# Decay scans in one piece, 112-partition loads and split weight checks in an RWKV and gMLP kernel on one core

## The chip, the core and the metric

The kernel runs on one core of a Trainium2 chip. TensorE (PE) multiplies matrices, VectorE (DVE), ScalarE (ACT) and GpSimd (POOL) work on rows of 128 partitions, and SyncE (SP) issues most of the transfers from and to HBM. Each engine takes its own instructions in a fixed order and waits on semaphores for the others. The metric is the device time of one execution in microseconds, the median of several.

## The reference

The first part is a recurrent attention with 4 batches, 8 heads, 768 positions and 48 features per head; the second is a gated MLP on its output. Cut to what matters:

```
for t in range(S):                                  # attention, per batch and head
    cur = outer(u * k[t], v[t])
    y[t] = r[t] @ (state + cur)
    state = w[t][:, None] * state + outer(k[t], v[t])
x = y with the heads side by side                   # 4 x 768 x 384
h = gelu(x @ w_in);  u, v = halves of h             # tanh form, 512 columns each
v = (v - mean) / sqrt(var + 1e-6) * g_ln
v = einsum('ts,bsd->btd', w_sg, v) + b_sg           # a 768 x 768 weight along the positions
out = x + (u * v) @ w_out
```

## The kernel before

The attention runs in 24 chunks of 128 positions (4 batches of 6). Two heads share a tile: one on the partitions 0 to 47, one on 64 to 111; the partitions 48 to 63 and 112 to 127 hold nothing of the data. Four such pairs lie side by side in the columns. For each chunk SP loads W (the decays, 517 columns: in each pair 128 decays and a guard column), KR (k and r), the values, and k by token.

`decays(n)` makes two scans from W. A scan is one instruction that carries a value from column to column: new = in0 * old + in1, or with the operations that it is given. The first (L568) runs from the back and gives the suffix products in Suf; it is reset at each pair by the ones in `resets`, a PSUM tile. Then the reciprocals of Suf's first columns are taken, one for each pair (L574), and a second scan (L576) multiplies the decays forward from them; for the first eight chunks (`early`) this is done in two halves, for the later ones (L581, L583) in one piece with the reciprocals in an fp32 tile D2 that is zero elsewhere. `decays` then multiplies R by W (L617), `decayed_k` multiplies K by Suf (L585), and `own_weights` makes the diagonal: a product K*R (L629), matmuls with `u_col` (L634), a copy and eight scaled identity tiles (L653). `scores` (L678), `masked` (L755), `products` (L685), `outputs` (L701, L712) and `state` follow on PE and DVE. The scores and the first products of a chunk lie in one PSUM tile `a_ps`.

The MLP's matmuls are written as three each, of a value's high and low part in fp32r (L950 to L952). `f64_weight` splits the weights into these parts (L1303 to L1328), and `f64_check` looks at the weights' high words again: SP loads a piece, ACT takes the Square (L1339) and the Sign (L1340), each with a sum over the columns. `range_check` does the like for the decays. `verdict` (L1260) turns the sums into one flag, by small DVE instructions and one matmul (L1278). Each engine reads the flag (L1431), and when it is bad, a slower path follows in the program.

Everything is cut into steps, written as generators. The table ORDER lists one step after another by a letter for its kind, a number for its chunk or piece, and the engine; the class Plan runs through the table, so it sets the order of each engine's instructions, the order of the loads in SP's queue too. Plan also estimates times, and where PE would wait for more than 0.4 us by its estimate, it calls `fill`, which puts warm-up matmuls (L481, on a constant tile) there.

Of the kernel before, what the change touches and what calls it, by code (L numbers as in the profile page):

```python
# [1610 lines left out]
```

## Time and profile before

| | us |
|---|---|
| median of 3 runs | 348.34 (347.72 to 348.59) |
| the profiled execution | 350.2 |
| its span | 348.4, and 1.8 around it |
| PE busy in the span | 340.0 (98%) |
| DVE, ACT, POOL busy | 273.0 (78%), 213.5 (61%), 148.2 (43%) |
| mean granted PE clock | 0.987 of full speed |

Times in the rows are microseconds from the start of the span unless marked ns. A busy PE may be at either level of its clock, and a warm-up matmul counts as busy as well; the predicted times are therefore set against the medians, and the stretches against the rows. 0.3% of the time is 1.05 us.

### The profile page before, as it was taken

The numbers are of one execution on the slowest core, as the hardware profiler recorded it, in microseconds if no ns is written. First come the engines' busy times: TensorE is split into PE (matmuls) and PEld (weight loads), VectorE is DVE, ScalarE is ACT, GpSimd is POOL, SyncE is SP. The second block draws the span as 40 slices with busy tenths as digits, with TensorE's granted clock in tenths as the row PEclk, the third lists the DMA queues.
The fourth block names the chain that finished last, engine by engine and source line by source line (L and its number), as shares of the span: only waits on it lengthen the run. The fifth ranks groups of instructions, "written<-read, shape, count | busy, mean of one in ns | idle before, by whom it ended". The sixth has DMA issues, their size and how long they took to land.

```text
span 348.4 us, 10988 instructions
## 1 busy us (share of the span) xinstructions
PE 340.0 (98%) x4453; PEld 313.9 (90%) x4453; DVE 273.0 (78%) x541; ACT 213.5 (61%) x564; POOL 148.2 (43%) x221
## 2 busy tenths in 40 slices
PE   7999999999999999999999999999999999999994
PEld 6887688899999899889999989999999889999993
DVE  6989999998999799777889796866746365767673
ACT  1579799972664477572313375372642689897982
POOL 7356343505524541453707445144323634448400
PEclk9699999999999999999999999999999999999998
DMA  7868995614256737235256345220365454636742
GB/s 287 300 225 288 345 337 186 189 56 158 85 170 215 236 130 236 68 105 206 76 163 202 115 147 197 96 100 36 119 205 173 155 182 164 232 125 192 201 147 95
DMA packets 28470, 60.46 MB, mean 174 GB/s; under 512 B 3456, under 2 KB 13184, under 8 KB 28416
## 3 DMA queue, kind: packets, MB, share of 16 engines
q1 hardware_dynamic: 28272, 59.63, 51.5%
q8 instruction: 36, 0.59, 0.7%
q14 instruction: 18, 0.15, 0.2%
q10 hardware_dynamic: 144, 0.10, 0.1%
HBM read 53.82 MB, written 4.72 MB: 168 GB/s over the span
## 4 chain that ended last, share of the span: by engine, by line
PE 91%; ACT 3%; POOL 2%; DMA 2%; DVE 1%; issue 0%; SPq 0%; POOLq 0%; ACTq 0%
PE m_ps L950 17%; PE m_ps L952 16%; PE m_ps L951 16%; PE resets L950 6%; PE resets L951 6%; PE resets L952 6%; PE a_ps L678 5%; PE y_ps L701 4%; PE y_ps L712 3%; PE y_ps L685 2%; DMA x<-y 2%; PE m_ps L481 2%; PE m_ps L1145 1%; PE a_ps L1145 1%; PE m_ps L724 1%; PE y_ps L1145 1%
## 5 line engine op out<-in xcount | busy, mean ns | idle before, releaser
L950 PE MATMUL m_ps<-wsgh,vn 128*128 128x384 f32 x114 | 39.1, 343 | 0.0
L952 PE MATMUL m_ps<-wsgh,vn 128*128 128x384 f32 x114 | 38.4, 337 | 0.0
L951 PE MATMUL m_ps<-wsgl,vn 128*128 128x384 f32 x114 | 38.3, 336 | 0.0
L653 ACT ACTIVATE a<-KR,own 128x64 f32<-128x64 f32 x120 | 30.4, 342 | 4.1 <-DVE own L647 4.0
L617 POOL TENSOR_TENSOR KR<-KR,W 128x512 f32<-128x512 f32 x18 | 21.8, 1216 | 23.6 <-DVE W L568 8.1
L950 PE MATMUL m_ps<-g,wouth 128*128 128x384 f32 x80 | 27.3, 341 | 0.0
L952 PE MATMUL m_ps<-g,woutl 128*128 128x384 f32 x80 | 26.9, 336 | 0.0
L951 PE MATMUL m_ps<-g,wouth 128*128 128x384 f32 x80 | 26.9, 336 | 0.0
L1050 ACT CAST g<-m_ps 128x384 fp32r<-128x384 f32 x21 | 9.9, 477 | 27.0 <-DVE m_ps L1048 27.0
L950 PE MATMUL m_ps<-xT,winh 128*128 128x384 f32 x75 | 25.9, 345 | 0.0
L952 PE MATMUL m_ps<-xT,winl 128*128 128x384 f32 x75 | 25.2, 336 | 0.0
L951 PE MATMUL m_ps<-xT,winh 128*128 128x384 f32 x75 | 25.2, 336 | 0.0
L987 POOL TENSOR_TENSOR st<-st,mhalf 128x1 f32<-128x1 f32 x24 | 14.7, 613 | 20.2 <-DVE g L1322 6.3
L678 PE MATMUL a_ps<-KR 64*64 64x128 f32 (+1 forms) x768 | 22.8, 255 | 0.0
L1046 DVE SCALAR_TENSOR_TENSOR m_ps<-m_ps,flat 128x384 f32<-128x384 f32 x21 | 13.0, 618 | 12.1 <-PE m_ps L952 11.3
L950 PEld LDWEIGHTS m_ps<-wsgh,vn 128*128 128x128 f32 x114 | 21.4, 188 | 0.6
L583 DVE TENSOR_TENSOR_SCAN W<-W,D 128x516 f32<-128x516 f32 x16 | 21.4, 1337 | 0.4
L952 PEld LDWEIGHTS m_ps<-wsgh,vn 128*128 128x128 f32 x114 | 21.4, 188 | 0.3 <-DVE vn L1002 0.3
L701 PEld LDWEIGHTS y_ps<-a,vtok 64*64 64x64 f32 x768 | 16.0, 134 | 6.2 <-issue 3.9
L951 PEld LDWEIGHTS m_ps<-wsgl,vn 128*128 128x128 f32 x114 | 21.4, 188 | 0.2
L701 PE MATMUL y_ps<-a,vtok 64*64 64x64 f32 x768 | 21.2, 224 | 0.0
L585 POOL TENSOR_TENSOR KR<-KR,W 128x512 f32<-128x512 f32 x12 | 14.8, 1231 | 14.3 <-PE m_ps L952 3.7
(374 smaller groups left out, 1095.7 us busy)
## 6 DMA issues: line engine op xcount, KB each, us to landing
KR<-in_kr SPq DMA_DIRECT2D x24, 512.0 KB, 4.5
RK<-in_ktok SPq DMA_DIRECT2D x20, 384.0 KB, 4.2
W<-in_wpad SPq DMA_DIRECT2D x24, 258.5 KB, 3.1
KR<-in_wpad SPq DMA_DIRECT2D x9, 517.0 KB, 3.8
vtok<-in_vtok SPq DMA_DIRECT2D x24, 192.0 KB, 3.8
out<-o SPq DMA_DIRECT2D x21, 192.0 KB, 2.7
vn<-in_w_in SPq DMA_DIRECT2D x6, 512.0 KB, 4.8
KR<-in_w_in SPq DMA_DIRECT2D x6, 512.0 KB, 4.1
```

The lines of the kernel that those rows point to most:

```text
L583: nc.vector.tensor_tensor_scan(W[:, 0:WL - 1], W[:, 0:WL - 1], D2[:, 0:WL - 1], 0.0, ALU.mult, ALU.add)
L585: engine[op.e].tensor_tensor(cols(x.R), cols(x.R), blocks(W, 0), ALU.mult)
L617: engine[op.e].tensor_tensor(cols(x.K), cols(x.K), blocks(x.Suf, 2), ALU.mult)
L653: nc.scalar.activation(a[:, j, p], eyes, AF.Copy, scale=o[:, j, p:p + 1])
L678: nc.tensor.matmul(ps_[64 * c_:64 * c_ + 64, j, p * C:p * C + (2 * T if c_ < turn else T)], x.K[rows, at:at + T], r_, start=True, stop=True)
L701: m = nc.tensor.matmul(place(y, j, q, r, c_), x.V[64 * c_:64 * c_ + 64, h * D - up(p, j):h * D - up(p, j) + 64], x.a.tile[64 * c_:64 * c_ ...
L950: nc.tensor.matmul(ps, lh, rh, start=(i == 0), stop=False)
L951: nc.tensor.matmul(ps, lh, rl, start=False, stop=False)
L952: nc.tensor.matmul(ps, ll, rh, start=False, stop=(i == n - 1))
L987: nc.gpsimd.tensor_tensor(rstd, var, c.mhalf, ALU.pow)
L1046: nc.vector.scalar_tensor_tensor(ps, ps, c.g[:, d:d + 1], c.b_bc[:, ts], ALU.mult, ALU.add)
L1145: nc.tensor.matmul(ps, x, y, start=False, stop=True, skip_group_check=True)
```

## The change

Three edits, and a new table ORDER.

The second scan of each chunk becomes one instruction. The reciprocals are written into the guard columns of W itself (one instruction for all four pairs), and the scan gets a constant zero as its second operand, one element repeated: `r_zero` from the PSUM tile `resets` for the early chunks, `d_zero` from the bf16 tile D1 for the later ones. D2 is free of the decays then.

The ten weight checks become twenty of half the columns, and load into D2 (pool `s_d2`), from chunk 8 on, instead of into the buffers of KR after the last chunk. Of the decay checks only the first loads in two parts, before the first three.

W and, from chunk 2 on, KR are loaded on 112 partitions; two small casts on ACT clear the partitions 96 to 127 of two KR buffers at the start, and the elementwise work on W, K, R and the decayed state runs on 112 partitions (LIVE). The first warm-up has 16 matmuls instead of 11, `fill` takes the bank that came free first and counts from the time at which it is free, and the own-weights from chunk 2 on have no filler of their own.

```diff
+LIVE = 64 + D
...
-WARM = (11, 80.0, 0.22)
+WARM = (16, 80.0, 0.22)
...
-            self.fill(t - gap, int((gap - 0.15) / WARM[2]))
+            self.fill(t - gap, t)
...
-    r_two = resets[:, 0:HQ]
+    r_zero = resets[:, 0:1].broadcast_to([128, WL - 1])
     r_one = resets.bitcast(BF16)[:, 2 * HQ + WL - C - 2:2 * HQ - C - 1:-1]
     D1 = per.tile([128, WL], BF16, name="D1")
+    d_zero = D1[:, 1:2].broadcast_to([128, WL - 1])
-    nc.vector.memset(D2, 0.0)
...
+    for _, t in s_kr.free[2:]:
+        nc.scalar.copy(t[96:128, 0:2 * NP * C], D1[96:128, 1:2].broadcast_to([32, 2 * NP * C]))
...
-    def fill(t, n):
-
-        free = [x for at, x in m_m.free if at <= t]
-        if free:
-            warm(ident, n, free[0])
+    def fill(t, end):
+
+        if m_m.free:
+            at, bank = min(m_m.free, key=lambda x: x[0])
+            warm(ident, max(0, int((end - max(at, t) - 0.15) / WARM[2])), bank)
...
-        nc.sync.dma_start(ch[n].W[:, 0:WL], wpad[steps[n]])
+        nc.sync.dma_start(ch[n].W[0:LIVE, 0:WL], wpad[steps[n]][0:LIVE])
...
+        rows = 128 if n < 2 else LIVE
...
-        nc.sync.dma_start(t[:, 0:2 * NP * C], kr[b, g])
+        nc.sync.dma_start(t[0:rows, 0:2 * NP * C], kr[b, g][0:rows])
...
-        W, Suf = x.W, x.Suf
-        nc.vector.tensor_tensor_scan(Suf[:, WL - 1:0:-1], W[:, WL - 1:0:-1], r_one if early else D1[:, WL - 1:0:-1], 0.0,
+        W, Suf = x.W[0:LIVE], x.Suf[0:LIVE]
+        nc.vector.tensor_tensor_scan(Suf[:, WL - 1:0:-1], W[:, WL - 1:0:-1], (r_one if early else D1[:, WL - 1:0:-1])[0:LIVE], 0.0,
                                      ALU.mult, ALU.add)
-        if early:
-            for i in range(2):
-                at = slice(i * HQ, (i + 1) * HQ)
-                yield Op({"DVE": 0.1}, after=[ch[n - 1].e_pre] if n else [])
-                nc.vector.reciprocal(r_two[:, 0:HQ:Q], Suf[:, i * HQ + 1:(i + 1) * HQ:Q])
-                op = yield Op({"DVE": 0.64}, done=x.e_pre if i else None)
-                nc.vector.tensor_tensor_scan(W[:, at], W[:, at], r_two, 0.0, ALU.mult, ALU.add)
-            if n == RESETS - 1:
-                m_m.free.append((op.seen, resets))
-        else:
-            yield Op({"DVE": 0.12}, after=[ch[n - 1].e_pre] if n else [])
-            nc.vector.reciprocal(D2[:, 0:WL - 1:Q], Suf[:, 1:WL - 1:Q])
-            yield Op({"DVE": 1.17}, done=x.e_pre, two=True)
-            nc.vector.tensor_tensor_scan(W[:, 0:WL - 1], W[:, 0:WL - 1], D2[:, 0:WL - 1], 0.0, ALU.mult, ALU.add)
+        yield Op({"DVE": 0.12})
+        nc.vector.reciprocal(W[:, 0:WL - 1:Q], Suf[:, 1:WL - 1:Q])
+        op = yield Op({"DVE": 1.17}, after=[ch[i].e_pre for i in range(n)] if n == RESETS - 1 else [], done=x.e_pre,
+                      two=not early)
+        nc.vector.tensor_tensor_scan(W[:, 0:WL - 1], W[:, 0:WL - 1], (r_zero if early else d_zero)[0:LIVE], 1.0, ALU.mult, ALU.add)
+        if n == RESETS - 1:
+            m_m.free.append((op.seen, resets))
         op = yield Op({"DVE": 0.61, "POOL": 1.18}, after=[x.e_KR, *x.own], done=x.e_r, two=True)
-        engine[op.e].tensor_tensor(cols(x.R), cols(x.R), blocks(W, 0), ALU.mult)
+        R = cols(x.R[0:LIVE])
+        engine[op.e].tensor_tensor(R, R, blocks(W, 0), ALU.mult)
...
-        two = n < 6
-        op = yield dma(258 if two else 516, take=[s_kr], after=[ch[N - 1].e_k], apart=two)
+        two = n < 2
+        op = yield dma(258 if two else 516, take=[s_kr], slack=2.0, after=[ch[N - 1].e_k], apart=two)
...
-            warm(ident, 2, m.tile)
+            warm(ident, 2 if n < 2 else 0, m.tile)
...
-        op = yield dma(n, take=[s_kr], after=[ch[N - 1].e_k])
+        op = yield dma(n, take=[s_d2], slack=3.0, after=[ch[RESETS].e_k])
...
-        yield Op({"ACT": 1.55}, free=[b], done=e_wchk[k])
+        yield Op({"ACT": 0.52 + n / 500}, free=[b], done=e_wchk[k])
...
-        plan.add(f64_check(k, w[1]))
+        for i in range(2):
+            n = w[1].shape[1] // 2
+            plan.add(f64_check(2 * k + i, w[1][:, i * n:(i + 1) * n]))
```

The table is new throughout. Of its places three are shown.

PE from the first warm-up on, before (`junk` and `same` are the warm-up's constants, KR_0_83 and KR_0_84 the first two chunks' tiles, `RK` the products for the own-weights):

```order
L481 MATMUL m_ps_0_132<-junk 128x128 x11
L481 MATMUL m_ps_0_132<-same 128x128 x2
L634 MATMUL m_ps_0_132<-u_col,RK_0_90 128x8 x4
L724 MATMUL m_ps_0_133<-same,KR_0_83 128x128 x4
L481 MATMUL m_ps_0_134<-same 128x128
L678 MATMUL a_ps_0_130<-KR_0_83 64x64 x16
L481 MATMUL m_ps_0_132<-same 128x128 x6
L481 MATMUL m_ps_0_134<-same 128x128 x2
L634 MATMUL m_ps_0_134<-u_col,RK_0_91 128x8 x4
```

And of the change:

```order
L484 MATMUL m_ps_0_132<-junk 128x128 x16
L484 MATMUL m_ps_0_132<-same 128x128 x2
L633 MATMUL m_ps_0_132<-u_col,RK_0_90 128x8 x4
L723 MATMUL m_ps_0_133<-same,KR_0_83 128x128 x4
L484 MATMUL m_ps_0_132<-same 128x128 x6
L484 MATMUL m_ps_0_134<-same 128x128 x2
L633 MATMUL m_ps_0_134<-u_col,RK_0_91 128x8 x4
L677 MATMUL a_ps_0_130<-KR_0_83 64x64 x16
L723 MATMUL m_ps_0_132<-same,KR_0_84 128x128 x4
L484 MATMUL m_ps_0_134<-same 128x128 x2
```

The own-weights of the second chunk (the second row with `u_col`) stood behind the first scores and two groups of fillers; now they stand ahead of the scores, behind all eight fillers.

DVE's first instructions on the data, before (a scan prints as SCALAR_TENSOR_TENSOR; W_0_81 and W_0_82 are the first two chunks' decays):

```order
L568 SCALAR_TENSOR_TENSOR W_0_81<-W_0_81,resets 128x516
L574 RECIPROCAL resets<-W_0_81 128x2
L576 SCALAR_TENSOR_TENSOR W_0_81<-W_0_81,resets 128x258
L574 RECIPROCAL resets<-W_0_81 128x2
L576 SCALAR_TENSOR_TENSOR W_0_81<-W_0_81,resets 128x258
L617 TENSOR_TENSOR KR_0_83<-KR_0_83,W_0_81 128x512
L568 SCALAR_TENSOR_TENSOR W_0_82<-W_0_82,resets 128x516
L1303 TENSOR_SCALAR vn_206<-vn_205 128x512
L1305 SCALAR_TENSOR_TENSOR vn_206<-vn_205,vn_206 128x512
L574 RECIPROCAL resets<-W_0_82 128x2
L576 SCALAR_TENSOR_TENSOR W_0_82<-W_0_82,resets 128x258
```

And of the change:

```order
L572 SCALAR_TENSOR_TENSOR W_0_81<-W_0_81,resets 112x516
L575 RECIPROCAL W_0_81<-W_0_81 112x4
L578 SCALAR_TENSOR_TENSOR W_0_81<-W_0_81,resets 112x516
L572 SCALAR_TENSOR_TENSOR W_0_82<-W_0_82,resets 112x516
L575 RECIPROCAL W_0_82<-W_0_82 112x4
L578 SCALAR_TENSOR_TENSOR W_0_82<-W_0_82,resets 112x516
L1303 TENSOR_SCALAR vn_203<-vn_202 128x512
L628 TENSOR_TENSOR RK_0_91<-KR_0_84 128x512
L1305 SCALAR_TENSOR_TENSOR vn_203<-vn_202,vn_203 128x512
L616 TENSOR_TENSOR KR_0_84<-KR_0_84,W_0_82 112x512
L1309 TENSOR_SCALAR vn_203<-vn_203 128x512
L583 TENSOR_TENSOR KR_0_84<-KR_0_84,W_0_82 112x512
```

Both chunks' scans now stand in a row, the second chunk's own-weights product (into RK_0_91) came over from POOL, and its product with W too, while the first chunk's product with W (into KR_0_83) is on POOL.

DVE's last instructions before the flag is read, before (`u` holds an output, `cnt` and `wchk` the verdict's sums):

```order
L1256 TENSOR_TENSOR u_0_123<-resets,x_0_111 128x384
L1256 TENSOR_TENSOR u_0_120<-m_ps_0_133,x_0_111 128x384
L1256 TENSOR_TENSOR u_0_121<-m_ps_0_132,x_0_111 128x192
L1256 TENSOR_TENSOR u_0_125<-m_ps_0_132,x_0_111 128x192
L1263 TENSOR_SCALAR chk<-chk 128x12
L1265 TENSOR_REDUCE cnt<-chk 128x1
L1268 TENSOR_SCALAR wchk<-wchk 128x10
L1271 TENSOR_SCALAR wchk<-wchk 128x6
L1271 TENSOR_SCALAR wchk<-wchk 128x4
L1273 TENSOR_REDUCE cnt<-wchk 128x1
L1275 TENSOR_TENSOR cnt<-cnt 128x1
L1280 TENSOR_SCALAR bad<-m_ps_0_134 1x1
```

And of the change:

```order
L1265 TENSOR_REDUCE cnt<-chk 128x1
L1052 TENSOR_TENSOR g_4602<-D_137,g_4602 128x384
L1268 TENSOR_SCALAR wchk<-wchk 128x20
L1271 TENSOR_SCALAR wchk<-wchk 128x12
L1271 TENSOR_SCALAR wchk<-wchk 128x8
L1256 TENSOR_TENSOR u_0_124<-m_ps_0_132,x_0_111 128x384
L1256 TENSOR_TENSOR u_0_121<-m_ps_0_133,x_0_111 128x384
L1273 TENSOR_REDUCE cnt<-wchk 128x1
L1256 TENSOR_TENSOR u_0_118<-m_ps_0_134,x_0_111 128x192
L1256 TENSOR_TENSOR u_0_120<-m_ps_0_134,x_0_111 128x192
L1275 TENSOR_TENSOR cnt<-cnt 128x1
L1280 TENSOR_SCALAR bad<-resets 1x1
```

Of the seven small instructions of the verdict in a row, all but the last now stand ahead of the last two outputs.

## Rows read from the trace of the kernel before

**Rows 1.** Windows of the span: busy us of each engine, granted PE clock, DMA share
```profile
9.00:20.00 11.00, 11.00 (x128) 9.39 (x127) 8.79 (x19) 6.27 (x23) 2.82 (x3) 0.73 0.84 295
20.00:40.00 20.00, 19.61 (x435) 15.26 (x434) 18.91 (x41) 16.57 (x55) 10.25 (x9) 1.00 0.84 275
40.00:60.00 20.00, 19.74 (x354) 15.59 (x353) 19.20 (x42) 19.42 (x56) 8.96 (x10) 1.00 0.84 287
60.00:80.00 20.00, 20.00 (x193) 18.08 (x193) 19.73 (x48) 15.78 (x42) 7.13 (x12) 1.00 0.37 114
80.00:100.00 20.00, 20.00 (x327) 19.08 (x326) 18.25 (x31) 11.69 (x40) 9.64 (x9) 1.00 0.43 147
```

**Rows 2.** What PE waits for: us in total, times, longest
```profile
PE m_ps L1278 <- DVE cnt L1275: 1.6, 1, 1.6
PE m_ps L481 <- POOL junk L458: 1.3, 1, 1.3
```

**Rows 3.** Timeline of PE, 0 to 24 us: start, us, instruction, passes
```profile
7.41 1.30 PE L634 MATMUL m_ps<-u_col,RK 128*128 128x8 f32 x8 [0.54 <-POOL RK L629]
...
9.45 0.63 PE L481 MATMUL m_ps<-same 128*128 128x128 f32 x2
...
11.08 3.78 PE L481 MATMUL m_ps<-same 128*128 128x128 f32 x16
14.65 1.08 PE L634 MATMUL m_ps<-u_col,RK 128*128 128x8 f32 x8
...
18.69 1.38 PE L481 MATMUL m_ps<-same 128*128 128x128 f32 x10
20.00 0.68 PE L685 MATMUL a_ps<-vtok,kt 64*64 64x48 f32 x32
20.61 0.71 PE L481 MATMUL m_ps<-same 128*128 128x128 f32 x4
```

**Rows 4.** Timelines of DVE, ACT and POOL, 3 to 22 us
```profile
5.10 0.17 DVE L574 RECIPROCAL resets<-W 128x2 f32<-128x2 f32 x1
...
6.24 0.69 DVE L576 TENSOR_TENSOR_SCAN W<-W,resets 128x258 f32<-128x258 f32 x1
...
9.14 0.49 DVE L1303 TENSOR_SCALAR vn<-vn 128x512 int32<-128x512 int32 x1
...
18.89 0.74 DVE L755 COPY_PREDICATED a<-mask,a_ps 128x512 f32<-128x512 uint8 x1 [2.07 <-ACT winh L1328]
...
15.77 0.17 ACT L372 COPY own<-m_ps 128x8 f32<-128x8 f32 x1 [4.13 <-PE m_ps L634]
...
16.31 2.02 ACT L653 ACTIVATE a<-KR,own 128x64 f32<-128x64 f32 x8
...
10.44 1.30 POOL L629 TENSOR_TENSOR RK<-KR 128x512 f32<-128x512 f32 x1 [1.09 <-DVE resets L574]
```

**Rows 5.** Groups of instructions by shape: busy us, mean ns, idle before
```profile
L583 DVE TENSOR_TENSOR_SCAN W<-W,D 128x516 f32<-128x516 f32 x16 | 21.4, 1337 | 0.4
...
L568 DVE TENSOR_TENSOR_SCAN W<-W,resets 128x516 f32<-128x516 f32 x8 | 9.8, 1220 | 0.9 <-DMA W<-in_wpad 0.9
...
L617 DVE TENSOR_TENSOR KR<-KR,W 128x512 f32<-128x512 f32 x6 | 4.1, 684 | 0.5 <-POOL RK L629 0.5
...
L1339 ACT ACTIVATE KR<-KR 128x512 f32<-128x512 f32 x6 | 4.0, 670 | 3.2 <-DMA KR<-in_w_in 3.2
...
L1339 ACT ACTIVATE KR<-KR 128x384 f32<-128x384 f32 x4 | 2.2, 561 | 5.0 <-DMA KR<-in_w_out 5.0
...
L1339 ACT ACTIVATION_READ_ACCUMULATOR KR<-KR 128x1 f32 x10 | 1.9, 190 | 0.0
```

**Rows 6.** Timeline of all engines at the end
```profile
343.64 0.16 DVE L1263 TENSOR_SCALAR chk<-chk 128x12 f32<-128x12 f32 x1
343.76 0.38 ACTq L1258 DMA_DIRECT2D out<-u  x1
...
344.47 0.16 DVE L1275 TENSOR_TENSOR cnt<-cnt 128x1 f32<-128x1 f32 x1
```

More of the change, by code (lines that the diff above doesn't have):

```diff
@@ L383, in rwkv_gmlp @@
     chk = cp.tile([128, B * NC // 2], F32, name="chk")
-    wchk = cp.tile([128, 2, 2 * KT + FT], F32, name="wchk")
+    wchk = cp.tile([128, 2, 2 * (2 * KT + FT)], F32, name="wchk")
     hmin, wmid, whalf = (cp.tile([128, 1], F32, name=x) for x in ("hmin", "wmid", "whalf"))
@@ L528, in load_w @@
     def load_w(n):
-        op = yield dma(258, take=[s_w], slack=SLACK["w"].get(n, 1.5), done=ch[n].e_W)
+        op = yield dma(226, take=[s_w], slack=SLACK["w"].get(n, 1.5), done=ch[n].e_W)
         ch[n].w, = op.got
@@ L532, in load_w @@
         ch[n].W, ch[n].Suf = (ch[n].w.tile[:, i * 520:(i + 1) * 520] for i in range(2))
-        nc.sync.dma_start(ch[n].W[:, 0:WL], wpad[steps[n]])
+        nc.sync.dma_start(ch[n].W[0:LIVE, 0:WL], wpad[steps[n]][0:LIVE])
     def load_kr(n):
         b, g = steps[n]
-        op = yield dma(512, take=[s_kr], slack=SLACK["kr"].get(n, 1.5), done=ch[n].e_KR)
+        rows = 128 if n < 2 else LIVE
+        op = yield dma(4 * rows, take=[s_kr], slack=SLACK["kr"].get(n, 1.5), done=ch[n].e_KR)
         ch[n].kr, = op.got
@@ L596, in range_check @@
             nc.sync.dma_start(t[:, 0], wpad[b, g])
-            yield dma(258)
+            yield dma(258, slack=2.0)
             nc.sync.dma_start(t[:, 1], wpad[b, g + 1])
@@ L611, in chunk_pc @@
         x.w.done(op.seen)
-        copy(op.e, x.pc.tile, x.Suf[:, 1:WL - 1:Q])
+        copy(op.e, x.pc.tile[0:LIVE], x.Suf[0:LIVE, 1:WL - 1:Q])
     def decayed_k(n):
@@ L629, in own_weights @@
             engine[op.e].tensor_tensor(t, x.K, x.R, ALU.mult)
-            op = yield Op({"PE": 1.3}, small=True, after=[e_uc], take=[m_m], free=[rk], n=16)
+            op = yield Op({"PE": 1.3 if n < 2 else 0.86}, small=True, after=[e_uc], take=[m_m], free=[rk], n=16)
             m, = op.got
-            warm(ident, 2, m.tile)
+            warm(ident, 2 if n < 2 else 0, m.tile)
             for p in range(NP):
@@ L789, in decayed @@
             for p in range(NP):
-                nc.scalar.activation(values(x.S2.tile)[:, p], before.S1.tile[:, p], AF.Copy, scale=x.pc.tile[:, p:p + 1])
-        else:
-            engine[op.e].tensor_tensor(values(x.S2.tile), before.S1.tile,
-                                       x.pc.tile.unsqueeze(2).broadcast_to([128, NP, D]), ALU.mult)
+                nc.scalar.activation(values(x.S2.tile)[0:LIVE, p], before.S1.tile[0:LIVE, p], AF.Copy,
+                                     scale=x.pc.tile[0:LIVE, p:p + 1])
+        else:
+            engine[op.e].tensor_tensor(values(x.S2.tile)[0:LIVE], before.S1.tile[0:LIVE],
+                                       x.pc.tile[0:LIVE].unsqueeze(2).broadcast_to([LIVE, NP, D]), ALU.mult)
         before.S1.done(op.seen)
@@ L1265, in verdict @@
         nc.vector.tensor_reduce(cnt[:, 0:1], chk, AX.X, ALU.add)
-        nw = 2 * KT + FT
+        nw = 2 * (2 * KT + FT)
         yield Op({"DVE": 0.1}, after=e_wchk)
         nc.vector.tensor_scalar(wchk[:, 0], wchk[:, 0], HMAX * HMAX, None, ALU.is_lt)
-        for k0, k1, n in ((0, 2 * KT, FF), (2 * KT, nw, DM)):
+        for k0, k1, n in ((0, 4 * KT, FF // 2), (4 * KT, nw, DM // 2)):
             yield Op({"DVE": 0.1})
@@ L1285, in rwkv_gmlp @@
     e_wout = [Event() for _ in range(FT)]
-    e_wchk = [Event() for _ in range(2 * KT + FT)]
+    e_wchk = [Event() for _ in range(2 * (2 * KT + FT))]
     e_u, e_uc = Event(), Event()
```

141 lines of the change are left out of this document (71 added, 70 removed).

## The prediction

> **What bounds the kernel now.** I read the windows first [rows 1]. From 80 us on the PE column stands at the full length of nearly every window, and in the three from 20 to 80 us it misses 0.39, 0.26 and 0.00 us. The list of PE's waits [rows 2] agrees: what PE waits for by name is 1.6 us behind the verdict's last vector instruction, 1.3 us for the first warm-up operand, and nothing larger. So time can be won in two places only: at the start, before PE is fed, and behind the last matmul. In the middle a change can only lose.
>
> The start holds more than the waits say, since PE fills its waiting with warm-up matmuls that compute nothing. The PE timeline [rows 3] shows it: 16 passes of L481 from 11.08 us for 3.78 us, 10 from 18.69 for 1.38 (two passes to each matmul of the code). In both stretches PE waits for the second chunk: its own-weights (L634) start only at 14.65, although POOL's product for them (L629) began at 10.44 and took 1.30 us [rows 4], so they could have started at 11.74. [...] Behind L634 follow ACT's copy of the own weights at 15.77 and its eight scaled copies from 16.31 for 2.02 us, then DVE's mask at 18.89, with DVE idle for 2.07 us just before [rows 4], then PE's first products at 20.00 [rows 3], which need the same PSUM tile that the mask reads.
>
> From 20 to 80 us DVE is busy 18.91, 19.20 and 19.73 of 20 us [rows 1]: there it is DVE that sets the pace, and PE does short attention work beside it.
>
> **The change, part by part.** *Scans.* Before, an early chunk pays after its first scan (1220 ns on average [rows 5]) twice a reciprocal (0.17) and a half scan (0.69); in the first chunk that is 1.83 us, from 5.10 to 6.24 + 0.69 = 6.93 [rows 4]. After, one reciprocal and one whole scan. The whole scan with a constant zero operand has no row; the nearest are the scan on `resets` in PSUM (1220) and the one over an fp32 tile in SBUF (1337) [rows 5]. I take 1220, because the new operand lies in PSUM too. A chunk is then 2 x (0.17 + 0.69) - (0.17 + 1.22) = 0.33 us cheaper (0.21 at 1337), eight chunks 2.6 us (1.7). If reading one element again and again made it slower, at 1.55 us a scan, the gain would be nothing. Against it, the new table hands DVE products that POOL did (an own-weights product and some products with the decays; L617, one of that shape, takes 0.68 us on DVE [rows 5]), so up to the first gate I estimate DVE's work to be equal within 0.5 us. The later 16 chunks save at most 16 x (1337 - 1220) = 1.9 us of DVE time, mostly where DVE has slack.
>
> *Start.* In the new order DVE does both chunks' scans back to back, and then the second chunk's own-weights product itself. From the reciprocal at 5.10: scan from about 5.3 to 6.5, the second chunk's first scan to 7.75, reciprocal and scan to about 9.2, one weight instruction (0.49, L1303 in [rows 4]), the product (0.68): ready at about 10.3. On PE the own-weights of the first chunk (7.41) and its transposes stay where they are; the filler of eight matmuls, 16 passes, follows at once at 9.45. Its passes cost (1.38 - 0.71) / 6 = 0.11 us at the full clock (ten passes against the four at 20.61) and (3.78 - 0.63) / 14 = 0.225 at the low one [rows 3]. So L634 of the second chunk starts at 9.45 + 1.8 = 11.2 or at 9.45 + 3.6 = 13.05, against 14.65. I take the full clock: five more warm-up matmuls (ten passes, 1.1 us at the full clock) close most of the gap in which PE stood idle before L634 at 7.41, and the low clock came behind that gap. The chain behind, with the durations of before, is 3.4 us earlier up to ACT's copies, which would end at 14.9. On DVE the mask now stands behind the next chunk's first scan, whose load I expect by the time that the scan's turn comes; that gives back about 0.6 us (half a scan). PE's first products then start at about 17.2, 2.8 earlier. As DVE sets the pace up to 80 us and its work is equal within 0.5 us, what the start wins stays won, less a part of those 0.5: **2.5 us**, bounds 0 (all of it lost again in DVE's stretch) and 4.5 (the 3.4, and the 1 us or so that DVE's shorter scans can give once it has no idle time).
>
> *Tail.* Behind the last half output DVE does seven instructions in turn, the first (L1263) at 343.64 and the last (L1275) at 344.47 [rows 6]; the matmul, the flag and the end hang on the last one. The new order puts six of them ahead of the last outputs, so that the last starts where the first did: 344.47 - 343.64 = 0.83 us earlier. The stores of the last outputs then come closer to the end: one store on ACT's queue takes 0.38 us to issue [rows 6], and the new order has two in a row there. I take **0.75 us**, bounds 0.4 (a store's issue later) and 0.83. The six are ready in time if the last check ends before the last output; the new order has it ahead of the last gates.
>
> *Checks.* Ten checks of 512 or 384 words become twenty of half the size. Each has two ACTIVATEs and two reads of the accumulator. By L1339 at 512 and 384 columns, a column costs (670 - 561) / 128 = 0.85 ns, so the fixed part of an ACTIVATE is 670 - 436 = 234 ns; with 190 ns for a read of the accumulator [rows 5], ten more checks cost ACT 20 x (0.234 + 0.190) = 8.5 us in all, and a half check takes 2 x 0.45 + 2 x 0.19 = 1.3 us. In ACT's new order the first stands behind the casts of the first four gates, the last near the end; I estimate 100 to 330 us. ACT is busy 11.69 of 20 us at 80 to 100 us [rows 1], so there is cover, and I take 0. Without cover each costs PE up to 1.3 us: a cast of the gated rows that PE needs stands behind it. On SP's queue each load waits for the check before it, because they share D2, and loads of later chunks stand behind that wait. Bounds 0 and +5 (four checks fully in the way).
>
> *112 partitions.* Vector and scalar instructions keep their columns, so I take 0 for them. The loads shrink by 24 x 32 KB and 22 x 64 KB, 2.2 MB. The DMA share is 0.84 from 9 to 20 us [rows 1], but W's first load and the two first kr loads that start the chain are not the ones that gain much: 0 as well, bound -0.3 us.
>
> Sum: 350.2 us of the profiled execution - 2.5 - 0.75 = 346.95; it stands 1.86 us above the median of 348.34, so the median comes to 348.34 - 3.25 = **345.1 us**.
>
> **The rivals.** (a) *The low clock stays* behind 8 us. For it: the narrow own-weights matmuls, 128x8, are unchanged, and the clock was low in the mixed window 9 to 20 us, fillers and all. Against it: the gap before them is smaller. L634 starts at 13.05; the start keeps 1.6, less 0.4 as above, and the tail's 0.75: 348.34 - 1.2 - 0.75 = 346.4. [...]
>
> (b) *DVE gives it all back.* For it: DVE is busy 57.84 of 60 us between 20 and 80 and does not get less work before the first gate. What is won at 20 us would then be lost by 80. Against it: DVE's own idle 2.07 us at 16.8 is gone. Only the tail stays: 347.6, which is within 0.3% of before, and 0.3% (1.05 us) is about what a measurement of this kernel can tell from no change.
>
> (c) *The checks get in the way*, which is the slower side. One mechanism: the ACT queue is in order, a check of 1.3 us stands ahead of a cast, and PE, which has no gap in the middle, waits. It decides from 3.25 / 1.3 = 2.5 checks on; with every fourth of twenty in the way it costs 6.5 us: 348.34 - 3.25 + 6.5 = 351.6. Against it: ACT has 8 us free in 20, and PE has matmuls of several gates to choose from, as far as the fixed order lets it.
>
> (d) *More than forecast*: the shorter scans act on a DVE that is now without idle time, and the start gives its upper bound 4.5: 348.34 - 4.5 - 0.75 = 343.1.
>
> (e) *The zero operand makes the scans slow* (over 1.55 us): the early chunks lose instead of winning, eight times the excess. At 1.9 us it is 8 x 0.35 = 2.8 us more in the stretch that DVE bounds: 348.34 - 3.25 + 2.8 = 347.9.
>
> **How the numbers follow.** Forecast 0.42, (a) 0.18, (b) 0.14, (c) 0.11, (d) 0.11, (e) 0.04. Faster by over 0.3% (below 347.3) are the forecast, (a) and (d): 0.71. Within 0.3%: (b), (e): 0.18. Slower: (c), 0.11. The range reaches from (d)'s time to above (b) and (e), 343.0 to 348.3, and leaves out (c) and about half of (d), 0.17. The likeliest case's own range, with the bounds of the tail and a part of the clock, is 344.2 to 346.4.
>
> **What would show it.** PE's own-weights of the second chunk at about 11.2 us and its first products near 17.2; the early whole scans near 1.22 us on 112 partitions and DVE without an idle time over 1 us between 10 and 20; PE without gaps from 80 us on; L1275 right behind the last half output. I am wrong if PE shows new waits behind ACT between 100 and 330 us, if the scan takes more than 1.4 us, if PE's idle time between 20 and 80 us grows by what the start won, or if the clock stays low behind 8 us.

## The result, and the profile after

The changed kernel is slower: 353.38 us (350.7 to 354.74, six executions) against 348.19 for the kernel before, a ratio of 1.0149 (95% interval 1.0107 to 1.019). Timed again beside the first experiments it took 352.02 against 348.45, 1.0108 (1.0067 to 1.0148). So it loses some 3.6 to 5.2 us where the prediction had it win 3.25. The profiled execution was the fastest of its six (350.7, span 349.0); its rows show less of the loss than most executions have.

The windows of the changed kernel, in the columns of [rows 1]:

```profile
9.00:20.00 11.00, 10.65 (x179) 8.59 (x179) 10.78 (x18) 8.07 (x29) 4.24 (x4) 1.00 1.03 305
20.00:40.00 20.00, 18.39 (x428) 13.61 (x421) 18.55 (x36) 17.16 (x55) 7.62 (x10) 1.00 1.00 298
40.00:60.00 20.00, 19.99 (x366) 16.48 (x357) 19.45 (x35) 16.69 (x49) 11.93 (x13) 1.00 0.79 214
60.00:80.00 20.00, 17.64 (x119) 15.33 (x120) 16.85 (x41) 15.60 (x39) 3.56 (x8) 1.00 0.53 167
80.00:100.00 20.00, 20.00 (x356) 19.05 (x355) 18.52 (x33) 14.54 (x50) 11.49 (x13) 1.00 0.43 136
```

PE, which missed 0.39 us between 20 and 40 and nothing between 60 and 80, now misses 1.61 and 2.36. From 80 us on it is full again, so the loss lies in the first 80 us. The DMA share there has risen to 1.00 while the GB/s have not risen in step, although fewer bytes are asked for: 0.84 went with 275 GB/s, now 1.00 with 298. The list of PE's waits, as [rows 2], names what it misses:

```profile
PE resets L950 <- ACT xT L373: 1.7, 1, 1.7
...
PE y_ps L711 <- ACT look L373: 0.9, 2, 0.6
PE resets L1278 <- DVE cnt L1275: 0.8, 1, 0.8
PE m_ps L939 <- DMA x<-y: 0.7, 1, 0.7
```

The timelines of the changed kernel, of PE at the start and then of the engines around the longest wait:

```profile
9.58 1.98 PE L484 MATMUL m_ps<-same 128*128 128x128 f32 x16
11.39 0.96 PE L633 MATMUL m_ps<-u_col,RK 128*128 128x8 f32 x8
...
18.14 0.68 PE L684 MATMUL a_ps<-vtok,kt 64*64 64x48 f32 x32 [0.34 <-DVE W L575]
...
57.33 4.44 POOL L987 TENSOR_TENSOR st<-st,mhalf 128x1 f32<-128x1 f32 x2
...
61.97 0.81 ACT L993 ACTIVATE v<-v,st 128x512 f32<-128x512 f32 x1 [4.32 <-POOL st L989]
...
63.09 0.51 ACT L373 CAST xT<-x 128x384 fp32r<-128x384 f32 x1
...
57.28 1.22 DVE L578 TENSOR_TENSOR_SCAN W<-W,resets 112x516 f32<-112x516 f32 x1
...
60.47 0.35 DVE L1309 TENSOR_SCALAR g<-g 128x384 int32<-128x384 int32 x1
63.63 0.56 DVE L945 TENSOR_TENSOR xT<-x,xT 128x384 fp32r<-128x384 f32 x1 [2.80 <-ACT xT L373]
...
63.65 0.50 PE L950 MATMUL resets<-winh,xT 128*128 128x512 f32 x1 [1.72 <-ACT xT L373]
```

Up to the second chunk's own-weights the start is what was forecast: they begin at 11.39 (forecast 11.2, before 14.65), behind filler passes of 0.12 us at the full clock (granted 1.00 from 9 to 20 us). The first products come at 18.14 (before 20.00), 0.9 us later than the 17.2 of the forecast. The second part of the timeline shows the longest wait. POOL computes two powers of one column each (L987: the 1/sqrt of the gated MLP's normalisation) in 4.44 us. Over the 24 powers of this execution the median is 0.55 us and the longest 3.92; in the profile of before the median is 0.57 and the longest 1.12. Beside them DVE runs without a pause from 57.28 to 60.82, and POOL is done 0.95 us after that. ACT waits 4.32 us for the statistic, its cast of xT stands behind the normalisation in its order, and PE waits for the cast.

### The profile page after: what moved, and what is told of

It reads as the page before. It is cut to its first block, busy times and chain, and to the rows that moved or that the text cites. A ratio compares the mean times of both kernels' runs of the same rounds, so it can differ in the third digit from the quotient of the medians.

```text
span 349.0 us, 11063 instructions
## 1 busy us (share of the span) xinstructions
PE 338.5 (97%) x4451; PEld 312.0 (89%) x4451; DVE 267.1 (77%) x524; ACT 228.2 (65%) x632; POOL 144.3 (41%) x216
## 4 chain that ended last, share of the span: by engine, by line
PE 85%; DMA 7%; issue 2%; ACT 2%; DVE 2%; SPq 1%; POOL 0%; POOLq 0%; ACTq 0%; DVEq 0%
PE m_ps L950 17%; PE m_ps L951 16%; PE m_ps L952 16%; PE a_ps L677 5%; PE resets L950 5%; PE resets L952 5%; PE resets L951 5%; DMA W<-in_wpad 4%; PE y_ps L700 3%; PE m_ps L484 3%; PE y_ps L711 3%; PE y_ps L684 2%; DMA KR<-in_kr 2%; DMA x<-y 2%; PE m_ps L1145 1%
## 5 line engine op out<-in xcount | busy, mean ns | idle before, releaser
L652 ACT ACTIVATE a<-KR,own 128x64 f32<-128x64 f32 x144 | 36.1, 337 | 0.6 <-DVE own L646 0.6
L987 POOL TENSOR_TENSOR st<-st,mhalf 128x1 f32<-128x1 f32 x24 | 18.1, 757 | 24.5 <-DVE RK L643 10.2
L950 PE MATMUL m_ps<-winh,xT 128*128 128x512 f32 x63 | 25.8, 409 | 0.0
L583 POOL TENSOR_TENSOR KR<-KR,W 112x512 f32<-112x512 f32 x12 | 14.3, 1191 | 27.3 <-DVE W L578 11.5
L951 PE MATMUL m_ps<-winl,xT 128*128 128x512 f32 x63 | 24.9, 394 | 0.0
L952 PE MATMUL m_ps<-winh,xT 128*128 128x512 f32 x63 | 24.8, 394 | 0.0
L950 PE MATMUL m_ps<-g,wouth 128*128 128x384 f32 x68 | 23.4, 344 | 0.0
L952 PE MATMUL m_ps<-g,woutl 128*128 128x384 f32 x68 | 22.7, 335 | 0.0
L951 PE MATMUL m_ps<-g,wouth 128*128 128x384 f32 x68 | 22.7, 334 | 0.0
L616 POOL TENSOR_TENSOR KR<-KR,W 112x512 f32<-112x512 f32 x15 | 17.9, 1192 | 11.2 <-DVE KR L583 4.2
L373 ACT COPY x<-y_ps 128x384 f32<-128x384 f32 x19 | 9.1, 477 | 19.2 <-PE y_ps L700 15.3
L950 PEld LDWEIGHTS m_ps<-wsgh,vn 128*128 128x128 f32 x111 | 20.8, 188 | 0.5
L578 DVE TENSOR_TENSOR_SCAN W<-W,D 112x516 f32<-112x516 f32 x16 | 20.7, 1296 | 0.2
```

The costliest lines, as they stand in the source:

```text
L578: nc.vector.tensor_tensor_scan(W[:, 0:WL - 1], W[:, 0:WL - 1], (r_zero if early else d_zero)[0:LIVE], 1.0, ALU.mult, ALU.add)
L583: engine[op.e].tensor_tensor(R, R, blocks(W, 0), ALU.mult)
L616: engine[op.e].tensor_tensor(K, K, blocks(x.Suf[0:LIVE], 2), ALU.mult)
L652: nc.scalar.activation(a[:, j, p], eyes, AF.Copy, scale=o[:, j, p:p + 1])
L950: nc.tensor.matmul(ps, lh, rh, start=(i == 0), stop=False)
L951: nc.tensor.matmul(ps, lh, rl, start=False, stop=False)
```

## The experiments

Two causes were suspected from these rows: (T1) the loads on 112 partitions are slower, not shorter, and (T2) the new table lets a small POOL instruction stand beside a dense DVE where ACT, and then PE, wait for it (L987 above; the next run showed a second place, L981). The rivals were the checks, the new scans and the verdict's new place. Of each edit the lines that bear on it are shown, of ORDER the entries that move. Before's median was 348.45, 348.38, 348.40 and 349.01 in the four comparisons.

**The changed kernel again**, no edit.

> The changed kernel once more, for a second profile: its first profiled execution (350.7) was the fastest of six (median 353.38). Every theory expects 352 to 355 here. What differs is where the profile shows the extra 2 to 4 us: by the theory of the narrow rows, in waits behind loads between 10 and 80 us, with a DMA share near 1.0 from 9 to 40 us again; by the theory that GpSimd's small instructions are held up, in one or two one-column instructions of 2 us or more on POOL.

Measured 352.02 (351.05 to 355.15). PE's list has a wait of 2.1 us for the one-element copy `look`, where the first profile had 0.9. Its timelines of POOL, ACT and PE:

```profile
36.32 2.67 POOL L981 TENSOR_SCALAR st<-st 128x1 f32<-128x1 f32 x1 [2.38 <-DVE vn L1303]
...
39.02 0.72 ACT L983 ACTIVATE junk<-v,st 128x512 f32<-128x512 f32 x1 [1.51 <-POOL st L981]
...
40.66 0.52 PE L711 MATMUL y_ps<-KR,S 64*64 64x64 f32 x20 [1.76 <-ACT look L373]
```

One column took POOL 2.67 us, and the same chain follows: ACT's square, the copy behind it, PE. In the table before this statistic was DVE's. In the first profile it took 0.23 us: it began at 35.91 with a DVE instruction that reads PSUM (L770, 35.88 to 36.24). Here it began at 36.32, 0.02 us ahead of a run of DVE work in SBUF that ended at 38.89, and POOL was done at 38.99.

**The 112 partitions undone** (W and KR loaded on 128; the vector work stays on 112), **and done alone** on the kernel before:

```diff
-        nc.sync.dma_start(ch[n].W[0:LIVE, 0:WL], wpad[steps[n]][0:LIVE])
+        nc.sync.dma_start(ch[n].W[:, 0:WL], wpad[steps[n]])
...
-        nc.sync.dma_start(t[0:rows, 0:2 * NP * C], kr[b, g][0:rows])
+        nc.sync.dma_start(t[:, 0:2 * NP * C], kr[b, g])
```

> The changed kernel with W and KR loaded on all 128 rows again, nothing else touched. If the loads on 112 rows are what makes transfers late (narrow rows), the DMA share from 9 to 40 us falls from 1.0 to about 0.85 and the time to 344 to 348. If the new table asks for too much too early whatever the rows are (rival), it stays at 352 to 355, or rises a little, since 2.2 MB more are moved.

> The kernel before with the 112 partitions alone: loads of W, and of KR for the chunks 2 to 19, on 112 rows, the two small casts at the start, and the elementwise work on 112 partitions; its own table, scans and checks. By narrow rows it is slower than before by 1 to 6 us, with later landings of W and KR. By the rival (the table) it is 347.5 to 348.8, no different.

The second also has the changed kernel's vector work on 112 partitions. Undone: 351.39 (350.19 to 351.95), 0.6 below the changed kernel of the same comparison, which the intervals (1.0052 to 1.0108 and 1.0067 to 1.0148) do not separate. Neither time of the expectation came: the DMA share fell, to 0.89 from 9 to 20 us and 0.90 from 20 to 40, but the time hardly followed. Done alone, with before's table: 352.16, a ratio of 1.0108 (1.007 to 1.0147), 3.7 us slower than before. The windows of that one (its profiled execution, 355.81, is the slowest of its six and shows more of the loss than most):

```profile
9.00:20.00 11.00, 9.56 (x128) 7.98 (x127) 9.70 (x19) 6.15 (x23) 4.05 (x3) 0.84 0.84 234
20.00:40.00 20.00, 20.00 (x436) 15.59 (x436) 19.42 (x42) 17.14 (x57) 10.82 (x9) 1.00 0.96 294
40.00:60.00 20.00, 15.73 (x282) 11.66 (x284) 14.80 (x30) 14.56 (x44) 7.84 (x10) 0.97 1.06 240
```

The same transfers, 2 MB shorter in all, keep the queues at 1.06 for 240 GB/s, where before moved 287 at 0.84 [rows 1], and both DVE (14.80) and PE (15.73) run dry. So T1 costs time in a kernel without the new table. That undoing it in the changed kernel gave back only 0.6 suggests that something else stood in the same place; the pair of versions further down, equal but for these loads, settles it.

**The weight checks left out** (loads and ACTIVATEs; their sums are set to constants):

```diff
-        nc.sync.dma_start(raw, src)
...
-        nc.scalar.activation(sq, sq, AF.Square, accum_out=wchk[:, 0, k:k + 1])
-        nc.scalar.activation(sq, sq, AF.Sign, bias=hmin, accum_out=wchk[:, 1, k:k + 1])
```

> The changed kernel without the weight checks: their twenty loads and forty ACTIVATEs are left out, and their sums are set to passing constants. If the checks in the middle are what costs the time, it falls by 3 us or more, to below 350.5. By narrow rows or by the table it moves by less than 1.5 us, since the checks only begin after 80 us.

Measured 352.04 (350.93 to 354.01), the changed kernel's time. The checks cost nothing that could be measured.

**Loads alone**, 512, 448 or 384 KB on 128, 112 or 96 partitions:

> The loads by themselves: eight stretches, each of twelve loads from HBM on SP's queue with nothing beside them, and a small read of each tile behind them; the work of the kernel is left out, the outputs are zeros. Stretches in order: KR rows of 4096 bytes on 128, 112, 96, 128, 112 partitions, then W rows of 2068 bytes on 128, 112, 96. If loads on 112 partitions are dear by themselves, a stretch of 112 takes as long as one of 128 or longer (12 x 512 KB = 6.3 MB at about 340 GB/s is 18.5 us), so GB/s fall by 12% or more. If a load only costs its bytes, 112 partitions take 0.875 of the time of 128, some 16.5 us, and 96 take 0.75.

The timeline of DVE, whose one-column copies read each buffer as it lands:

```profile
17.17 0.15 DVE L385 COPY sums<-X 128x1 f32<-128x1 f32 x1 [1.00 <-DMA X<-in_kr]
...
18.45 0.15 DVE L385 COPY sums<-X 128x1 f32<-128x1 f32 x1 [1.00 <-DMA X<-in_kr]
...
26.01 0.15 DVE L385 COPY sums<-X 112x1 f32<-112x1 f32 x1 [1.33 <-DMA X<-in_kr]
...
27.63 0.15 DVE L385 COPY sums<-X 112x1 f32<-112x1 f32 x1 [1.34 <-DMA X<-in_kr]
...
46.32 0.15 DVE L385 COPY sums<-X 96x1 f32<-96x1 f32 x1 [1.30 <-DMA X<-in_kr]
...
47.90 0.15 DVE L385 COPY sums<-X 96x1 f32<-96x1 f32 x1 [1.30 <-DMA X<-in_kr]
```

512 KB on 128 partitions come every 1.28 us, 448 KB on 112 every 1.62, 384 KB on 96 every 1.58. Dropping an eighth of the rows makes a load 1.27 times as long. From 14 to 22 us, on 128 partitions, 405 GB/s are moved, from 24.4 to 34 us, on 112, 284; the expectation put 340 there, where the two fastest slices on before's page have 345 and 337. Further stretches give 1.28 for 128 rows again and 1.63 to 1.80 for 112. Loads of W's row length (2068 bytes) come every 0.68 us on 128 partitions and every 0.79 on 112.

**The first statistic back on DVE**, with the loads on 128 partitions (one entry of the table):

```diff
-K0P K0P K0A K0G H4P x3P
+K0P K0P K0A K0D H4P x3P
```

> The changed kernel with 128-row loads, and besides with the first statistics instruction of the first value piece (L981, one column) on DVE, as it was before, instead of on POOL. If GpSimd's one-column instructions are held up beside a dense DVE (2.67 us instead of 0.2 in two profiles) and that holds up ACT and PE, the wait of PE behind ACT's look copy near 39 us (1.8 and 2.2 us in these profiles) goes, and the time falls from 351.4 to 349.3 to 350.5. If that wait only stands in for something else that is late, PE waits there as long for another, and the time stays at 351 to 352.

Measured 350.02 (349.2 to 351.71), 1.4 below 351.39. PE's wait of L711 for ACT's `look` (2.2 us with wide loads alone) is gone from its list. That for xT is 0.9 (0.2 with wide loads alone), and a new one of 1.6 us stands behind a product on POOL (L616).

**The scans of the first eight chunks alone, and the verdict's place alone**, on the kernel before:

```diff
-            for i in range(2):
-                at = slice(i * HQ, (i + 1) * HQ)
...
+            nc.vector.reciprocal(W[:, 0:WL - 1:Q], Suf[:, 1:WL - 1:Q])
...
+            nc.vector.tensor_tensor_scan(W[:, 0:WL - 1], W[:, 0:WL - 1], r_zero, 1.0, ALU.mult, ALU.add)
```

> The kernel before with the second scan of the early chunks in one piece and the reciprocals in the guard columns; its table is the same but for the two steps less in each of eight chunks. By the prediction's step the early chunks save 0.33 us of DVE each where DVE sets the pace: 346 to 347.7. If the new zero operand is dear, or DVE is not what bounds there, 348 to 349.

```diff
-u21P u21D u21S u22P u22D u22S u23P u23D u23S u23D u23A M0D
-M0D M0D M0D M0D M0D M0D M0P M0D
+u21P M0D M0D M0D M0D M0D u21D u21S u22P u22D u22S M0D u23P u23D u23S u23D
+u23A M0D M0P M0D
```

> The kernel before with six of the verdict's seven small DVE instructions ahead of the last outputs, nothing else. By the prediction's step the end comes 0.75 us earlier: 347.4 to 347.9. If the last stores set the end, 348.2 to 348.6.

Measured 348.73, 1.0008 (0.9984 to 1.0032), and 348.74, 1.0011 (0.9993 to 1.0029): neither gains. In the first the new scan takes 1226 ns, and the eight chunks' second scans with their reciprocals fall from 13.7 to 11.2 us of DVE's time in all, so the operand is not dear; 2.5 us less work for DVE is not 2.5 us less time. The sixteen later scans were not tried alone. The profile of the second, whose start is before's, instruction for instruction, shows something else. Its timeline of PE:

```profile
10.59 2.73 PE L481 MATMUL m_ps<-same 128*128 128x128 f32 x16
13.16 0.96 PE L634 MATMUL m_ps<-u_col,RK 128*128 128x8 f32 x8
...
18.39 0.68 PE L685 MATMUL a_ps<-vtok,kt 64*64 64x48 f32 x32
```

Against [rows 3] the same passes take 2.73 us and not 3.78, and the first products start at 18.39 and not 20.00. The execution of before that was profiled had a longer low stretch of the clock than most (mean 0.987; granted 0.50 from 9 to 14 us and 1.00 from 15 to 21, in all 0.73 from 9 to 20, against 0.86 here). In the four comparisons 76 executions of before are listed: six have a mean clock of 0.986 or 0.987 and take 350.07 to 350.50, the other 70 have 0.990 or more and a median of 348.41.

**DVE paused beside the powers**, on 128 partitions with the statistic on DVE: the split of x, which DVE must wait for anyway, is put ahead of six DVE steps, and ACT's cast for it directly behind the normalisation.

```diff
-K2G k8D e7D k6D k8D k6D k8D j6A C4A C4D j8A
+K2G C4A C4D k8D e7D k6D k8D k6D k8D j6A j8A
```

> The changed kernel with loads on 128 partitions, the first statistic on VectorE, and, new here, VectorE paused while GpSimd computes the two powers near 57 us: the low half of the x split stands ahead of the six weight-cutting and r-product steps instead of behind them, and ScalarE's x cast directly behind the normalisation that waits for the powers. Theory: with VectorE silent the two powers take 1.1 us and not 4.4, ScalarE's wait of 3.5 us shrinks to under 1, TensorE's waits at 62 and 65 us (1.1 and 0.8 us) go, and the time is 348.2 to 349.0 (350.0 less 1.0 to 1.8). Rival (the powers are late by themselves, or the loss is the start's and is only shown there): powers still over 3 us, or time unchanged within 0.3 us of 350.0.

Measured 348.65 (348.26 to 349.93), a ratio to before of 1.0014 (1.0 to 1.0028). Its timelines of POOL, ACT and DVE, and its window:

```profile
57.03 1.09 POOL L987 TENSOR_TENSOR st<-st,mhalf 128x1 f32<-128x1 f32 x2
...
58.32 0.82 ACT L993 ACTIVATE v<-v,st 128x512 f32<-128x512 f32 x1 [0.16 <-POOL st L989]
...
59.57 0.56 DVE L945 TENSOR_TENSOR xT<-x,xT 128x384 fp32r<-128x384 f32 x1 [1.37 <-ACT xT L373]
...
60.00:80.00 20.00, 19.93 (x190) 17.84 (x182) 19.58 (x47) 14.79 (x38) 2.49 (x6) 1.00 0.56 179
```

With nothing but the scan beside them the two powers take 1.09 us, DVE idles 1.37 us and not 2.80, and PE misses 0.07 us from 60 to 80. T2 holds.

**The cast moved, without the pause**, and **the pause with the narrow loads**:

```diff
-a7A K1G K1A t5S
+a7A K1G C4A K1A t5S
...
-K2G k8D e7D k6D k8D k6D k8D j6A C4A C4D j8A
+K2G k8D e7D C4D k6D k8D k6D k8D j6A j8A
```

> The same kernel without that pause: ScalarE's x cast moved ahead of the normalisation that waits for the powers, and the low half of the x split to the middle of VectorE's steps, so that TensorE's next gate does not hang on the powers. Theory: the powers stay at about 4 us, since VectorE is as dense as before, but TensorE's wait at 62 us goes: 348.5 to 349.3. Rival: the wait only moves to the next operand that hangs on the powers (the normalised v), and the time stays within 0.3 us of 350.0.

> The changed kernel with its loads on 112 partitions as they are, the first statistic on VectorE and the pause near 57 us. It separates the two causes: against the version on 128 partitions of the same order the difference is the price of the narrow loads where nothing else holds the start up. If the narrow loads are the larger cause: over 350.5, at least 1.5 us above the wide version. If GpSimd's late statistics are: within 0.7 us of the wide version, near 349.

The first took 350.33 (349.64 to 352.35): the powers stay at 4.37 us and PE waits 1.3 us for `u` instead (0.6 without the edit), which stands behind the normalisation too; its profile also has a wait of 1.2 us for `look` again. It is the powers that have to be done earlier, not one of those who wait. The second took 351.23 (349.4 to 353.29): with both places of POOL mended the narrow loads cost 351.23 - 348.65 = 2.6 us, in two versions that differ by these loads alone and whose intervals, 1.0054 to 1.0116 and 1.0 to 1.0028, lie apart. T1 holds.

**POOL's power beside single kinds of DVE work**, measured by itself twice; in the first the kinds came out mixed.

> A measurement by itself: only the statistic's power on GpSimd (128x1, six in a row, each reading the one before) beside seven different neighbours on VectorE: nothing, scans over 512 columns with one operand in PSUM, int32 shift-and-mask over 384 columns, int32 two-operand steps over 384 columns, fp32 products with both operands in SBUF, fp32 products with one operand in PSUM, and fp32 one-operand products. All of the kernel's own work is left out and the outputs are zeros. Theory (a small GpSimd instruction is held up by a VectorE that runs without pause): six powers take about 3.3 us beside nothing (0.55 each) and much more, 8 us or up to the end of VectorE's run, beside at least one of the dense neighbours. Rival (the powers of the changed kernel were late for another reason, a semaphore or the instruction's own dispatch): 0.55 us each beside all of them.

> The measurement of GpSimd's powers again, now with one kind of VectorE neighbour in each phase of about 5.5 us, in this order: a clear of 512 columns alone, scans with a PSUM operand, int32 shift-and-mask in place, int32 two-operand steps, fp32 products with both operands in SBUF, fp32 products with one operand in PSUM, products and shifts in turn, scans and shifts in turn. All of the kernel's own work is left out and the outputs are zeros. Theory (the hold needs VectorE instructions that read two SBUF operands, back to back): six powers take 3.3 to 4 us beside scans and PSUM products, and over 5 us, with one power over 1.5 us, beside SBUF products or the mixture with shifts. Rival (any dense VectorE run holds them alike, by chance of the moment): the excess is spread over the phases without regard to the operands.

In the first, six powers beside DVE products and shifts in turn fall into these two windows (POOL alone):

```profile
17.41:21.48 4.07, 4.07 (x1) 1.00 0.00 0
21.50:24.65 3.15, 2.75 (x5) 1.00 0.00 0
```

One power stood for 4.07 us; DVE stopped at 21.1, and the other five took 0.55 each. The second, POOL's timeline, one row of six powers for each neighbour in the order of the expectation, the last beside nothing:

```profile
3.68 3.69 POOL L388 TENSOR_TENSOR st<-st,half 128x1 f32<-128x1 f32 x6 [3.24 <-DVE st L386]
7.64 3.68 POOL L388 TENSOR_TENSOR st<-st,half 128x1 f32<-128x1 f32 x6 [0.27 <-DVE st L386]
14.84 4.69 POOL L388 TENSOR_TENSOR st<-st,half 128x1 f32<-128x1 f32 x6 [3.52 <-DVE st L386]
24.05 4.05 POOL L388 TENSOR_TENSOR st<-st,half 128x1 f32<-128x1 f32 x6 [4.52 <-DVE st L386]
32.12 4.68 POOL L388 TENSOR_TENSOR st<-st,half 128x1 f32<-128x1 f32 x6 [4.01 <-DVE st L386]
40.30 3.68 POOL L388 TENSOR_TENSOR st<-st,half 128x1 f32<-128x1 f32 x6 [3.50 <-DVE st L386]
48.48 6.68 POOL L388 TENSOR_TENSOR st<-st,half 128x1 f32<-128x1 f32 x6 [4.49 <-DVE st L386]
57.24 3.88 POOL L388 TENSOR_TENSOR st<-st,half 128x1 f32<-128x1 f32 x6 [2.09 <-DVE st L386]
64.77 3.68 POOL L388 TENSOR_TENSOR st<-st,half 128x1 f32<-128x1 f32 x6 [3.64 <-DVE st L386]
```

Scans and products that read PSUM hold nothing up (3.68, as beside nothing). Work whose operands all lie in SBUF does: 4.05 to 4.69 for one kind, 6.68 for products and shifts in turn, the kind of run that stands beside L981 and L987. The product shows it best, 4.68 with both operands in SBUF and 3.68 with one in PSUM. So in this measurement it is where the operands lie that decides. That there must be two, as the expectation had it, is not so: the shifts have one and take 4.69, while products alone stay under the 5 us that it gave. How long a hold lasts differs with the same two neighbours (4.07 us for one power in the first, 6.68 / 6 = 1.11 for each in the second), and what sets that stays open.

The hold of 4.07 us outlasts any one DVE instruction there (0.68 at most), so POOL did not wait for a single one of them to end. By what means DVE holds POOL up, no run here shows.

**Other row counts**, and **the next late POOL product on DVE** (on the version with the pause; PE waited 1.4 us for it at 42 us):

> Loads alone again, twelve of each kind, in this order: 128 rows in one transfer, 120, 112, 112 as 64 and 48, 128 as 64 and 64, 64, 32, 128. All of the kernel's own work is left out and the outputs are zeros. [...] Rival (only the odd row count matters): 64 and 48 rows together take 1.1 to 1.2 us, less than 128 rows in one.

```diff
-d4G K0G K0G e5G K0G D4D f5D D4D f5D z4P
+d4G K0G K0G K0G D4D f5D D4D e5D f5D z4P
```

> The changed kernel with wide loads, the first statistic on VectorE and the pause, and the decayed k product of one chunk near 42 us on VectorE, ahead of its second scan, in place of GpSimd, where it took 2.5 us and TensorE waited 1.4 us for it. Theory (the start's win is lost to the next thing that GpSimd does late): that wait goes and the time is 347.0 to 348.0 us, below the kernel before. Rival (VectorE, full between 20 and 60 us, sets the pace there and takes the win whatever GpSimd does): within 0.4 us of 348.65.

DVE's timeline of the loads, 64 and 48 rows in two transfers, and then 64 rows:

```profile
87.61 0.15 DVE L383 COPY sums<-X 112x1 f32<-112x1 f32 x1 [1.70 <-DMA X<-in_kr]
...
89.60 0.15 DVE L383 COPY sums<-X 112x1 f32<-112x1 f32 x1 [1.71 <-DMA X<-in_kr]
...
124.35 0.15 DVE L383 COPY sums<-X 64x1 f32<-64x1 f32 x1 [0.96 <-DMA X<-in_kr]
...
125.57 0.14 DVE L383 COPY sums<-X 64x1 f32<-64x1 f32 x1 [0.95 <-DMA X<-in_kr]
```

In two transfers 112 rows take 1.99 us, longer than in one (1.75 here), and 128 rows as 64 and 64 take 2.17; 64 rows take 1.22, hardly less than all 128, and 32 rows 0.64. The 256 KB of 64 rows in 1.22 us are 215 GB/s and the 128 KB of 32 rows in 0.64 us are 205, where 128 rows in one transfer moved 411 (15.5 to 21 us of this measurement) and 112 moved 262 (49 to 58 us). So a load on half the rows won next to nothing here, and what makes one on 112 rows longer than one on 128 stays open.

The product is the decayed k, L616 here and L617 in the kernel before, where L585 is the product with W (the description above has these two lines exchanged). The version with it on DVE took 348.46 (348.2 to 351.23), 1.0001 (0.9977 to 1.0025), level with before and not to be told from the pause alone; the expectation of 347.0 to 348.0 missed. That wait is gone; another takes its place, from PE's list:

```profile
PE y_ps L711 <- ACT look L373: 1.3, 1, 1.3
```

No version here beats the kernel before.

## Why the prediction was wrong, point by point

**112 partitions.** "The loads shrink by … 2.2 MB … 0 as well, bound -0.3 us." This is the step that failed first, with the wrong sign. A load on 112 partitions takes 1.62 us where one on 128 takes 1.28, and between 9 and 60 us the queues are near full. In the kernel before, the edit with its vector work costs 3.7 us, in the changed one the loads cost 2.6 with the order mended and 0.6, within the noise, without. The bytes were counted and the time for them was not read from any row; [rows 1] had a queue at 0.84 and so no room for a slower load.

**Scans and table.** "Up to the first gate I estimate DVE's work to be equal within 0.5 us" counted the table's moves by what they add to DVE. Not counted was what then stands beside POOL's small instructions: one statistic that the new table moved to POOL (1.4 us by undoing it) and two powers that were POOL's before and now stand beside a dense DVE (another 1.4, 350.02 - 348.65). The early scan itself is as predicted, 1224 ns on 112 partitions with the zero operand, and worth nothing alone; the premise behind its price, that DVE sets the pace up to 80 us, is not borne out by 2.5 us less of DVE's work that gained nothing. The sixteen later ones take 1296 ns and not 1220, some 0.7 us of DVE's time in all where at most 1.9 was put.

The two causes hide each other. Undone first, either is worth little: 0.6 us for the loads, 0.8 for POOL's places (351.23), neither clear of the noise. Undone second each is worth far more, 2.7 us for POOL's places and 2.6 for the loads. Wide loads and two changes of the order undo the whole loss.

**Start.** The own-weights came within 0.2 us of the forecast, the clock was full (granted 1.00 from 9 to 20 us), and rival (a) did not come in the profiles with the new table; the low stretch is not the same in every execution of before, whose mean clocks go from 0.986 to 1.000. (The time of that rival should have been some 346.9: the "0.4 as above" that it takes off stands nowhere above, where 0.6 and 0.3 are taken off.) What failed is the step behind the own-weights, "that gives back about 0.6 us". ACT's and DVE's timelines of the changed kernel:

```profile
12.97 2.02 ACT L652 ACTIVATE a<-KR,own 128x64 f32<-128x64 f32 x8
...
16.25 1.22 DVE L572 TENSOR_TENSOR_SCAN W<-W,resets 112x516 f32<-112x516 f32 x1
17.38 0.70 DVE L754 COPY_PREDICATED a<-mask,a_ps 128x512 f32<-128x512 uint8 x1
```

ACT's copies end at 14.99, as forecast (14.9). The mask that needs them starts at 17.38, 2.4 us later, since DVE, without a pause up to there, does weight instructions and the next chunk's whole scan first. In the execution of the kernel before's start with first products at 18.39 the mask waits 0.6 us behind the copies (16.71 to 17.28), with DVE idle for 0.45 us ahead of it and not the 2.07 that the prediction counted on. So a lead of 1.77 us at the own-weights (11.39 against 13.16) is 0.25 at the first products (18.14 against 18.39). The other profiles with the new table have their first products between 17.95 and 19.28.

The size was wrong against the median for a second reason: the profiled execution "stands 1.86 us above the median", and the sum took 2.5 off that median, although 1.61 us of that excess (20.00 - 18.39) was there at the first products, in the stretch with the low clock (0.73 from 9 to 20 us), where the changed kernel was granted 1.00. "What the start wins stays won" could not be tested with so little won. With both causes mended the time is only level with before (348.65, 348.46); PE still waits behind ACT or POOL between 20 and 60 us, and DVE is busy 20.00 of 20 us from 20 to 40. That is near rival (b), under the two losses: DVE gives back what was won, but earlier than it was put. What takes up the 0.62 us of the tail as well (below) is not shown.

**Tail.** PE waits 0.8 us for the verdict's last vector instruction and not 1.6 [rows 2]. PE's last output matmul in the timeline of before, and then of the changed kernel:

```profile
342.73 0.34 PE L952 MATMUL m_ps<-g,woutl 128*128 128x384 f32 x1
```

```profile
343.95 0.34 PE L952 MATMUL m_ps<-g,woutl 128*128 128x384 f32 x1
```

From there to the end of the span it was 348.4 - 342.73 = 5.67 us and is 349.0 - 343.95 = 5.05: a gain of 0.62 where 0.75 was forecast. With that edit alone PE's wait was 1.0 us, and no gain could be measured in the medians.

**Checks.** Nothing, as taken. Rival (c) gave a time near the measured one (351.6) by a mechanism that did not occur: PE was busy all 160 us from 80 to 240, and 59.66 of 60 from there to 300 (before 59.76). That its time came near is luck.

## What to carry to other kernels

Count a transfer by a row for its shape, not by its bytes: on 112 partitions it took 1.62 us here and on 128 1.28, and with the queues at 0.84 that was time (2.6 us). When an order changes, look at what stands beside each small GpSimd instruction that another engine waits for; a pause of VectorE there, of time that it idled anyway, was worth 1.4 us here (350.02 - 348.65). Set a gain against the median only after asking whether the profiled execution's excess over the median is the same stretch.

## What the hardware showed unexpectedly

A one-column GpSimd instruction of 0.55 us took up to 4.07 us beside VectorE work with all operands in SBUF, and six of them took no longer than beside nothing (3.68 us) when VectorE's scans or products read one operand from PSUM. Loads on 120 partitions came every 1.96 us (30.08 and 32.04 in the timeline of the second load measurement), slower than on 112 (1.75), 96 (1.58) or 128 (1.28).
